# A product with w_out in seven half-size products, the activation as one ScalarE function, and a new order of the start

## The chip, the cores and the metric

One core of one Trainium2 chip runs the kernel. The metric is the device time of the whole kernel in microseconds (us), the median of several runs. All runs told here were in the fast state (executions can fall into a second, slower one, and then aren't compared). Engines are named as the profile names them: PE is TensorE, PEld its weight loads, DVE VectorE, ACT ScalarE, POOL GpSimd, SP the engine that issues most transfers.

## The reference, cut to what matters

```python
# x: (8, 3008, 256); w_in: (256, 2048); w_out: (2048, 256)
X = np.fft.fft(np.fft.fft(x, axis=1), axis=2).real        # mixing over rows, then over columns
h = X.reshape(24064, 256) @ w_in
g = h * (1.0 / (1.0 + np.exp(-1.702 * h)))                 # the quick GELU
out = g @ w_out
```

## The kernel before

The transform over the rows is done as a first stage (94 x 32 points: VectorE or GpSimd fold rows onto each other, TensorE multiplies, ScalarE copies the result out), a shuffle through DRAM, and a second stage. The transform over the columns is folded into w_in. Then 384 steps follow (8 batches, 48 each): a step makes 128 hidden units for 512 rows and their mirrored rows, and adds their product with w_out to eight accumulators. The product runs two steps behind (LAG). The first stage of the next batch is spread over the steps in 8 chunks. Below, the code is cut; `...` marks what is left out.

```python
def hidden(t):                                   # one step
    nc.tensor.matmul(pa, wcs[0][:, fs], pq[:, 0, :]); nc.tensor.matmul(pb, wcs[1][:, fs], pq[:, 1, :])
    nc.scalar.copy(v[:], pa[:])
    nc.vector.tensor_tensor(h[:, 0, :], v[:], pb[:], op=ALU.add)              # the rows
    nc.vector.scalar_tensor_tensor(dif[:], nb[:], af2[:, f:f+1], pb[:], ...)
    nc.vector.tensor_tensor(<h[:, 1, :] backwards>, v, dif, op=ALU.add)       # the mirrored rows
    nc.scalar.activation(sg[:], h[:], ACTF.Sigmoid, scale=1.702)
    nc.vector.tensor_tensor(h[:], h[:], sg[:], op=ALU.mult)

def product(t):                                  # 8 matmuls of 256 columns into 4 banks
    for sg in range(2):
        for g in range(4):
            nc.tensor.matmul(pot[2*sg + g//2][:, g % 2, :], lhsT=h[:, sg, g*128:(g+1)*128], rhs=wo[:, f, :], ...)
    # ... after 16 steps: 4 copies out of the banks, 8 stores

for t in range(n + LAG):
    if t < n: hidden(t)
    if t >= LAG: product(t - LAG)
    for fn, args in extra.get(t, ()): fn(*args)  # first stage of the next batch (a chunk every 2 steps), second stage, ...
```

In every stretch of trace shown below, an engine works through its own instructions in program order: one that could start stands behind one that can't.

## Time and profile before

| | before |
|---|---|
| time | 2282.53 us (2282.07 to 2284.93, 4 runs) |
| first step of the main loop | 122.8 us |
| a step without extras | 5.17 us |
| a batch (from one psr matmul, a small one that comes once a batch, to that of the next) | 265.5 us |

The prediction shows the lines for these. Two groups of the page of the kernel before show what the change wants to take off VectorE; columns are line, engine, operation, tiles, shapes, count, then busy us, mean ns, and the idle time before them:

```profile
L294 DVE TENSOR_TENSOR h<-h,sg 128x1024 f32<-128x1024 f32 x384 | 483.6, 1259 | 455.6 <-ACT sg L293 455.6
L293 ACT ACTIVATE sg<-h 128x1024 f32<-128x1024 f32 x384 | 405.7, 1057 | 970.2 <-DVE h L290 970.1
```

The multiply is VectorE's costliest group. Yet VectorE is busy for 60% of the span and ScalarE for 33%, and both wait for each other (455.6 and 970.1 us).

### The profile page before, as it was taken

The numbers are of one execution on the slowest core, as the hardware profiler recorded it, in microseconds if no ns is written. First come the engines' busy times: TensorE is split into PE (matmuls) and PEld (weight loads), VectorE is DVE, ScalarE is ACT, GpSimd is POOL, SyncE is SP. The second block draws the span as 40 slices with busy tenths as digits, with TensorE's granted clock in tenths as the row PEclk, the third lists the DMA queues.
The fourth block names the chain that finished last, engine by engine and source line by source line (L and its number), as shares of the span: only waits on it lengthen the run. The fifth ranks groups of instructions, "written<-read, shape, count | busy, mean of one in ns | idle before, by whom it ended". The sixth has DMA issues, their size and how long they took to land.

```text
span 2280.3 us, 21583 instructions
## 1 busy us (share of the span) xinstructions
PE 2167.9 (95%) x8496; PEld 1574.4 (69%) x8496; DVE 1358.0 (60%) x1657; ACT 748.8 (33%) x970; POOL 254.5 (11%) x277
## 2 busy tenths in 40 slices
PE   3358999999999999999999999999999999999999
PEld 2136777777777777777777777777777777777776
DVE  4255666656666556656566566565666566665665
ACT  1122333333333333333333333333333333333332
POOL 3124000310005000040003100050000400000000
PEclk9669999999999999999999999999999999999999
DMA  9700400004000130004000040001300020000000
GB/s 306 209 19 0 111 17 19 19 1 128 19 1 19 36 92 19 19 1 117 11 19 19 1 128 19 1 19 46 82 19 19 1 74 0 19 19 0 18 19 18
DMA packets 40721, 96.92 MB, mean 43 GB/s; under 512 B 4402, under 2 KB 28722, under 8 KB 38254
## 3 DMA queue, kind: packets, MB, share of 16 engines
q1 hardware_dynamic: 39536, 91.26, 14.6%
q10 hardware_dynamic: 1084, 4.29, 0.5%
q8 instruction: 66, 1.08, 0.2%
q14 instruction: 35, 0.29, 0.0%
HBM read 58.31 MB, written 48.78 MB: 47 GB/s over the span
## 4 chain that ended last, share of the span: by engine, by line
PE 89%; DVE 4%; DMA 3%; issue 2%; ACT 1%; POOL 1%; SPq 0%; DVEq 0%; ACTq 0%; POOLq 0%
PE po L305 55%; PE pa L280 14%; PE pb L281 14%; PE ps L171 2%; PE ps L197 2%; PE psn L205 1%; DMA raw<-in_moe_w_in_dram 1%; ACT sg L293 1%; DMA Xr<-in_x_dram 1%; DMA Td<-t 1%; DVE h L290 1%; DVE h L287 1%; DVE dif L289 1%; DVE os L316 0%; DVE m L240 0%
## 5 line engine op out<-in xcount | busy, mean ns | idle before, releaser
L305 PEld LDWEIGHTS po<-wo,h 128*128 128x128 f32 x6144 | 1168.0, 190 | 335.6 <-issue 134.0
L305 PE MATMUL po<-wo,h 128*128 128x256 f32 x6144 | 1393.0, 380 | 6.2 <-DVE h L294 5.1
L294 DVE TENSOR_TENSOR h<-h,sg 128x1024 f32<-128x1024 f32 x384 | 483.6, 1259 | 455.6 <-ACT sg L293 455.6
L293 ACT ACTIVATE sg<-h 128x1024 f32<-128x1024 f32 x384 | 405.7, 1057 | 970.2 <-DVE h L290 970.1
L287 DVE TENSOR_TENSOR h<-v,pb 128x512 f32<-128x512 f32 x384 | 263.8, 687 | 372.3 <-PE pb L281 369.6
L280 PE MATMUL pa<-pq,wcs 128*128 128x512 f32 x768 | 398.6, 601 | 0.0
L281 PE MATMUL pb<-pq,wcs 128*128 128x512 f32 x768 | 394.0, 595 | 1.6 <-DVE dif L289 1.6
L286 ACT COPY v<-pa 128x512 f32<-128x512 f32 x384 | 224.6, 585 | 296.6 <-PE pa L280 290.6
L289 DVE SCALAR_TENSOR_TENSOR dif<-nb,af,pb 128x512 f32<-128x512 f32 x384 | 284.6, 741 | 0.0
L290 DVE TENSOR_TENSOR h<-v,dif 128x512 f32<-128x512 f32 x384 | 268.9, 700 | 13.1
L281 PEld LDWEIGHTS pb<-pq,wcs 128*128 128x128 f32 x768 | 146.5, 191 | 187.6 <-issue 181.7
L280 PEld LDWEIGHTS pa<-pq,wcs 128*128 128x128 f32 x768 | 141.0, 192 | 38.1 <-issue 20.5
L151 POOL TENSOR_TENSOR e<-xt 94x254 f32<-94x254 f32 x7 | 5.0, 719 | 1387.2 <-DVE h L290 920.6
L171 PE MATMUL ps<-xt,w 94*96 94x256 f32 x240 | 70.2, 419 | 12.6 <-POOL xt L163 8.3
L160 POOL TENSOR_TENSOR xt<-xt 94x510 f32<-94x510 f32 (+1 forms) x59 | 73.4, 1244 | 4.6
L162 POOL TENSOR_TENSOR xt<-xt 94x254 f32<-94x254 f32 (+1 forms) x59 | 68.7, 1165 | 4.6
L176 ACT COPY t<-ps 96x512 f32<-96x512 f32 x64 | 37.2, 581 | 94.0 <-PE ps L171 93.5
L171 PEld LDWEIGHTS ps<-xt,w 94*96 94x96 f32 x240 | 42.0, 180 | 28.4 <-POOL xt L163 9.9
L261 PE MATMUL psw<-wst,small 128*128 128x512 f32 x32 | 18.7, 739 | 43.1 <-POOL wst L246 43.1
L197 PEld LDWEIGHTS ps<-small,t 128*128 128x128 f32 x384 | 51.1, 194 | 6.6 <-DVE t L189 4.2
L197 PE MATMUL ps<-small,t 128*128 128x128 f32 x384 | 51.7, 278 | 4.0 <-DVE t L189 4.0
L199 ACT COPY pq<-ps 128x512 f32<-128x512 f32 x48 | 28.1, 585 | 58.2 <-PE ps L197 58.2
(44 smaller groups left out, 344.2 us busy)
## 6 DMA issues: line engine op xcount, KB each, us to landing
out_dram<-os SPq DMA_DIRECT2D x176, 128.0 KB, 2.1
Td<-t SPq DMA_DIRECT2D x8, 1536.0 KB
t<-Td SPq DMA_DIRECT2D x8, 1536.0 KB, 7.8
Xr<-in_x_dram SPq DMA_DIRECT2D x8, 1410.0 KB, 14.4
xt<-in_x_dram SPq DMA_DIRECT2D x7, 1280.0 KB
xt<-Xr SPq DMA_DIRECT2D x7, 1200.0 KB
raw<-in_moe_w_out_dram SPq DMA_DIRECT2D x4, 1024.0 KB, 21.1
raw<-in_moe_w_in_dram ACTq DMA_DIRECT2D x3, 1024.0 KB
```

Of the source, the lines that this page charges most:

```text
L160: eng.tensor_tensor(low, low, free(t[:], up + D - 1, [-D, n], [-1, D - 1]), op=ALU.add)
L171: nc.tensor.matmul(ps[0:96, o:o + D], lhsT=w1[:, jj, :], rhs=t[:, NB - jj, :], start=True, stop=True)
L197: nc.tensor.matmul(ps[:, g * 128:(g + 1) * 128], lhsT=t4[:, 4 * blk + g, cs * H:(cs + 1) * H], rhs=m2[:, cs, :], start=True, stop=True)
L280: nc.tensor.matmul(pa[:], lhsT=wcs[0][:, fs], rhs=pq[:, 0, :], start=True, stop=True)
L281: nc.tensor.matmul(pb[:], lhsT=wcs[1][:, fs], rhs=pq[:, 1, :], start=True, stop=True)
L286: nc.scalar.copy(v[:], pa[:])
L287: nc.vector.tensor_tensor(h[:, 0, :], v[:], pb[:], op=ALU.add)
L289: nc.vector.scalar_tensor_tensor(dif[:], nb[:], af2[:, f:f + 1], pb[:], op0=ALU.mult, op1=ALU.subtract)
L290: nc.vector.tensor_tensor(free(h[:], 512 + NB - 1, [NB, 16], [-1, NB]), v[:].rearrange("p (a k) -> p a k", k=NB), dif[:].rearrange("p (a k ...
L293: nc.scalar.activation(sg[:], h[:], ACTF.Sigmoid, scale=1.702)
L294: nc.vector.tensor_tensor(h[:], h[:], sg[:], op=ALU.mult)
L305: nc.tensor.matmul(pot[2 * sg + g // 2][:, g % 2, :], lhsT=h[:, sg, g * 128:(g + 1) * 128], rhs=wo[:, f, :], start=(f == 0 and g % 2 == 0) ...
```

## The change

The intent: Strassen's scheme in Winograd's form takes seven half-size products for eight, so TensorE streams an eighth less for the product with w_out. A step now takes two blocks of 128 hidden units for half of the rows. Four sums of the activations are needed per step (s1, s3 on GpSimd, s2, s4 on VectorE), four of w_out once (wt), and seven additions when a sum ends, now every 8 steps. To make room in VectorE's time, one Gelu with the sigmoid form replaces Sigmoid and multiply. To make room in memory, the first stage writes over x. The start is put in another order: rows are turned in DRAM during the loop, a batch at a time, and not all at once, the last piece of w_in is loaded early, the first is converted before the first stage. The core of the diff:

```diff
-        nc.scalar.activation(sg[:], h[:], ACTF.Sigmoid, scale=1.702)
-        nc.vector.tensor_tensor(h[:], h[:], sg[:], op=ALU.mult)
+        nc.scalar.activation(h[:], h[:], ACTF.Gelu_apprx_sigmoid)
+
+    def sums(t):                                  # called for t - 1 in hidden(t), after the first half of h
+        a11, a12, a21, a22 = h[:, 0, 0, :], h[:, 0, 1, :], h[:, 1, 0, :], h[:, 1, 1, :]
+        nc.gpsimd.tensor_tensor(s1, a21, a22, op=ALU.add)
+        nc.gpsimd.tensor_tensor(s3, a11, a21, op=ALU.subtract)
+        nc.vector.tensor_tensor(s2, s1, a11, op=ALU.subtract)
+        nc.vector.tensor_tensor(s4, a12, s2, op=ALU.subtract)
 
     def product(t):
-            ... 8 matmuls of 256 columns
+        plan = ((0, 0, h[:, 0, 0, :], wo[:, p, 0, :]), (0, 1, s[:, 1, :], wt[:, p, 1, :]),
+                ... )                             # seven, each as two matmuls of 128 columns
+        ...                                       # when a sum ends:
+        nc.scalar.copy(c1[:], m1)
+        for out, i0, i1, o in ((u2[:], c1[:], m6, ALU.add), ... ):      # seven
+            nc.vector.tensor_tensor(out, i0, i1, op=o)
...
-    for b in range(1, B):
-        turn(b, 17, 32)                           # at the start
+        if b + 2 < B:
+            at(t0 + 10, turn, b + 2, 17, 32)      # in the loop
...
-                at(t0 + 3 + 2 * c, stage1, b + 1, c, nc.gpsimd)
+                at(t0 + 7 + 2 * c, stage1, b + 1, c, nc.gpsimd)
```

(Left out: the early load and conversion of w_in, the in-place copy of the first stage, the split of the shuffle, buffer counts.)

More of the change, by code (lines that the diff above doesn't have):

```diff
@@ L93 @@
     xp = ctx.enter_context(tc.tile_pool(name="xp", bufs=1, space=SB))
-    tp = ctx.enter_context(tc.tile_pool(name="tp", bufs=2, space=SB))
+    tp = ctx.enter_context(tc.tile_pool(name="tp", bufs=1, space=SB))
     pqp = ctx.enter_context(tc.tile_pool(name="pqp", bufs=2, space=SB))
@@ L112 @@
     wcs = [const.tile([128, DF], F32, tag=f"wcs{i}", name=f"wcs{i}") for i in range(2)]
-    wo = const.tile([128, NF, D], F32, tag="wo", name="wo")
+    wo = const.tile([128, NF // 2, 4, H], F32, tag="wo", name="wo")
+    wt = const.tile([128, NF // 2, 4, H], F32, tag="wt", name="wt")
     af2 = const.tile([128, NF], F32, tag="af2", name="af2")
@@ L118, in bank @@
         return psm.tile([128, 512], F32, tag="mm", name=name)
-    xt, t1t, t4t, pqt, nbt = {}, {}, {}, {}, {}
+    xt, t4t, pqt, nbt = {}, {}, {}, {}
     def turn(b, m0, m1):
@@ L129, in load_x @@
     def load_x(b, pieces=((0, 16),)):
-        t = xt[b] = xp.tile([NA, NB, D], F32, tag="x", name="xt")
+        t = xt[b] = xp.tile([96, NB, D], F32, tag="x", name="xt")
         src = x[b].rearrange("(p j) d -> p j d", j=NB)
@@ L144, in stage1 @@
     def stage1(b, c, eng):
-        t = xt[b]
+        full = xt[b]
+        t = full[0:NA]
         if c == 0:
             e = sp.tile([NA, 2, D], F32, tag="v", name="e")
-            fwd, rev = free(t[:], 1, [16 * D, 2], [1, H - 1]), free(t[:], D - 1, [16 * D, 2], [-1, H - 1])
+            fwd, rev = free(t, 1, [16 * D, 2], [1, H - 1]), free(t, D - 1, [16 * D, 2], [-1, H - 1])
             eng.tensor_tensor(e[:, :, 1:H], fwd, rev, op=ALU.add)
-            eng.tensor_copy(free(e[:], 0, [D, 2], [H, 2]), free(t[:], 0, [16 * D, 2], [H, 2]))
+            eng.tensor_copy(free(e[:], 0, [D, 2], [H, 2]), free(t, 0, [16 * D, 2], [H, 2]))
             eng.tensor_tensor(e[:, :, H + 1:D], fwd, rev, op=ALU.subtract)
@@ L156, in stage1 @@
         at, up = lo * D, (NB - lo) * D
-        ends = free(t[:], up, [-D, n], [H, 2])
-        eng.tensor_tensor(ends, ends, free(t[:], at, [D, n], [H, 2]), op=ALU.add)
-        low = free(t[:], at + 1, [D, n], [1, D - 1])
-        eng.tensor_tensor(low, low, free(t[:], up + D - 1, [-D, n], [-1, D - 1]), op=ALU.add)
-        fwd, rev = free(t[:], at + 1, [D, n], [1, H - 1]), free(t[:], at + D - 1, [D, n], [-1, H - 1])
-        eng.tensor_tensor(free(t[:], up + 1, [-D, n], [1, H - 1]), fwd, rev, op=ALU.add)
-        eng.tensor_tensor(free(t[:], up + H + 1, [-D, n], [1, H - 1]), fwd, rev, op=ALU.subtract)
-        if c == 0:
-            t1t[b] = tp.tile([96, 16, D], F32, tag="t1", bufs=1, name="t1")
+        ends = free(t, up, [-D, n], [H, 2])
+        eng.tensor_tensor(ends, ends, free(t, at, [D, n], [H, 2]), op=ALU.add)
+        low = free(t, at + 1, [D, n], [1, D - 1])
+        eng.tensor_tensor(low, low, free(t, up + D - 1, [-D, n], [-1, D - 1]), op=ALU.add)
+        fwd, rev = free(t, at + 1, [D, n], [1, H - 1]), free(t, at + D - 1, [D, n], [-1, H - 1])
+        eng.tensor_tensor(free(t, up + 1, [-D, n], [1, H - 1]), fwd, rev, op=ALU.add)
+        eng.tensor_tensor(free(t, up + H + 1, [-D, n], [1, H - 1]), fwd, rev, op=ALU.subtract)
         ps = bank("ps1")
@@ L175, in stage1, with spill, fill @@
                 nc.tensor.matmul(ps[0:96, c0:c1], lhsT=w1[:, l1, :], rhs=e[:, 1, c0:c1], start=False, stop=True)
-        nc.scalar.copy(t1t[b][:, 2 * c:2 * c + 2, :].rearrange("p j d -> p (j d)"), ps[0:96, :])
-    def shuffle(b):
+        nc.scalar.copy(full[:, 2 * c:2 * c + 2, :].rearrange("p j d -> p (j d)"), ps[0:96, :])
+    def spill(b):
+        nc.sync.dma_start(out=Td[b].rearrange("(p j) d -> p j d", j=16), in_=xt[b][:, 0:16, :])
+    def fill(b):
         t4 = t4t[b] = tp.tile([128, NG, D], F32, tag="t4", name="t4")
-        nc.sync.dma_start(out=Td[b].rearrange("(p j) d -> p j d", j=16), in_=t1t[b][:])
         nc.sync.dma_start(out=t4[:], in_=Td[b].rearrange("(a p) d -> p a d", p=128))
@@ L226, in bounds @@
         hi = raw[key][:, :, 1].bitcast(F32)
-        g = sp.tile([128, 1024], F32, tag="sg", name="g")
+        g = sp.tile([128, 1024], F32, tag="s", bufs=3, name="g")
         m = cv.tile([128, 1024], F32, tag="m", bufs=2, name="m")
@@ L254, in round_out @@
     def round_out(n):
-        rounded(wo[:, 4 * n:4 * n + 4, :].rearrange("p f n -> p (f n)"), ("out", n))
+        ps = slice(2 * n, 2 * n + 2)
+        rounded(wo[:, ps].rearrange("p f q n -> p (f q n)"), ("out", n))
+        b11, b12, b21, b22 = (wo[:, ps, q, :] for q in range(4))
+        t1, t2, t3, t4 = (wt[:, ps, q, :] for q in range(4))
+        for out, i0, i1 in ((t1, b12, b11), (t2, b22, t1), (t3, b22, b12), (t4, t2, b21)):
+            nc.gpsimd.tensor_tensor(out, i0, i1, op=ALU.subtract)
     def fold_w(n):
@@ L269, in nyquist_weights @@
         nc.vector.tensor_scalar(af2[:], ps[:, 0:NF], scalar1=2.0, scalar2=None, op0=ALU.mult)
-    steps = [(b, blk, f) for b in range(B) for blk in range(NBLK) for f in range(NF)]
-    ht, pot = {}, {}
+    NP = NF // 2
+    steps = [(b, blk, hh, p) for b in range(B) for blk in range(NBLK) for hh in range(2) for p in range(NP)]
+    ht, st, pot, ot = {}, {}, {}, {}
     def hidden(t):
-        b, blk, f = steps[t]
-        pq, nb, fs = pqt[b, blk], nbt[b, blk], slice(f * 128, (f + 1) * 128)
+        b, blk, hh, p = steps[t]
+        pq, nb, ks = pqt[b, blk], nbt[b, blk], slice(hh * 256, hh * 256 + 256)
         pa, pb = bank("pa"), bank("pb")
-        nc.tensor.matmul(pa[:], lhsT=wcs[0][:, fs], rhs=pq[:, 0, :], start=True, stop=True)
-        nc.tensor.matmul(pb[:], lhsT=wcs[1][:, fs], rhs=pq[:, 1, :], start=True, stop=True)
-        h = ht[t] = hp.tile([128, 2, 512], F32, tag="h", name="h")
+        for ps, cs in ((pa, 0), (pb, 1)):
+            for i in range(2):
+                f = 2 * p + i
+                nc.tensor.matmul(ps[:, i * 256:(i + 1) * 256], lhsT=wcs[cs][:, f * 128:(f + 1) * 128],
+                                 rhs=pq[:, cs, ks], start=True, stop=True)
+        h = ht[t] = hp.tile([128, 2, 2, 256], F32, tag="h", name="h")
         v = sp.tile([128, 512], F32, tag="v", name="v")
-        sg = sp.tile([128, 2, 512], F32, tag="sg", name="sg")
+        dif = sp.tile([128, 512], F32, tag="dif", name="dif")
         nc.scalar.copy(v[:], pa[:])
-        nc.vector.tensor_tensor(h[:, 0, :], v[:], pb[:], op=ALU.add)
-        dif = sp.tile([128, 512], F32, tag="dif", name="dif")
-        nc.vector.scalar_tensor_tensor(dif[:], nb[:], af2[:, f:f + 1], pb[:], op0=ALU.mult, op1=ALU.subtract)
+        nc.vector.tensor_tensor(h[:, 0].rearrange("p f k -> p (f k)"), v[:], pb[:], op=ALU.add)
+        sums(t - 1)
+        for i in range(2):
+            c = slice(i * 256, i * 256 + 256)
+            f = 2 * p + i
+            nc.vector.scalar_tensor_tensor(dif[:, c], nb[:, ks], af2[:, f:f + 1], pb[:, c],
+                                           op0=ALU.mult, op1=ALU.subtract)
         nc.vector.tensor_tensor(free(h[:], 512 + NB - 1, [NB, 16], [-1, NB]),
@@ L292, in hidden @@
                                 dif[:].rearrange("p (a k) -> p a k", k=NB), op=ALU.add)
-        nc.scalar.activation(sg[:], h[:], ACTF.Sigmoid, scale=1.702)
-        nc.vector.tensor_tensor(h[:], h[:], sg[:], op=ALU.mult)
+        nc.scalar.activation(h[:], h[:], ACTF.Gelu_apprx_sigmoid)
+    def sums(t):
+        if not 0 <= t < len(steps):
+            return
+        h = ht[t]
+        s = st[t] = sp.tile([128, 4, 256], F32, tag="s", bufs=3, name="s")
+        a11, a12, a21, a22 = h[:, 0, 0, :], h[:, 0, 1, :], h[:, 1, 0, :], h[:, 1, 1, :]
+        s1, s2, s3, s4 = (s[:, q, :] for q in range(4))
+        nc.gpsimd.tensor_tensor(s1, a21, a22, op=ALU.add)
+        nc.gpsimd.tensor_tensor(s3, a11, a21, op=ALU.subtract)
+        nc.vector.tensor_tensor(s2, s1, a11, op=ALU.subtract)
+        nc.vector.tensor_tensor(s4, a12, s2, op=ALU.subtract)
@@ L296, in product @@
     def product(t):
-        b, blk, f = steps[t]
-        if f == 0:
+        b, blk, hh, p = steps[t]
+        if p == 0:
             for n in range(4):
-                pot[n] = pso.tile([128, 2, D], F32, tag=f"o{n}", name=f"po{n}")
-        h = ht.pop(t)
-        for sg in range(2):
-            for g in range(4):
-                nc.tensor.matmul(pot[2 * sg + g // 2][:, g % 2, :], lhsT=h[:, sg, g * 128:(g + 1) * 128],
-                                 rhs=wo[:, f, :], start=(f == 0 and g % 2 == 0), stop=(f == NF - 1),
-                                 skip_group_check=True)
@@ L308, in product @@
-        if f < NF - 1:
-            return
-        for sg in range(2):
-            o = op.tile([128, 4, D], F32, tag="os", name="os")
-            for i in range(2):
-                dst = free(o[:], 3 * D - 2 * i * D, [-D, 2], [1, D]) if sg else o[:, 2 * i:2 * i + 2, :]
-                eng = nc.scalar.copy if i else nc.vector.tensor_copy
-                eng(dst, pot[2 * sg + i][:])
-            store(b, blk, sg, o)
+                pot[n] = pso.tile([128, 2, 2, H], F32, tag=f"o{n}", name=f"po{n}")
@@ new lines, in product @@
+        h, s = ht.pop(t), st.pop(t)
+        plan = ((0, 0, h[:, 0, 0, :], wo[:, p, 0, :]), (0, 1, s[:, 1, :], wt[:, p, 1, :]),
+                (1, 0, h[:, 0, 1, :], wo[:, p, 2, :]), (1, 1, s[:, 2, :], wt[:, p, 2, :]),
+                (2, 0, s[:, 0, :], wt[:, p, 0, :]), (2, 1, s[:, 3, :], wo[:, p, 3, :]),
+                (3, 0, h[:, 1, 1, :], wt[:, p, 3, :]))
+        for n, i, lhs, rhs in plan:
+            for q in range(2):
+                nc.tensor.matmul(pot[n][:, i, q, :], lhsT=lhs[:, q * 128:(q + 1) * 128], rhs=rhs,
+                                 start=(p == 0 and i == 0 and q == 0), stop=(p == NP - 1), skip_group_check=True)
@@ new lines, in product @@
+        if p < NP - 1:
+            return
+        (m1, m6), (m2, m7), (m5, m3), (m4, _) = ((pot[n][:, 0], pot[n][:, 1]) for n in range(4))
+        if hh == 0:
+            for sg in range(2):
+                ot[sg] = op.tile([128, 4, D], F32, tag="os", name="os")
+        c1, u2, u3, u4 = (op.tile([128, 2, H], F32, tag=f"u{n}", bufs=1, name=f"u{n}") for n in range(4))
+        dst = [ot[0][:, 2 * hh:2 * hh + 2, :], free(ot[1][:], (3 - 2 * hh) * D, [-D, 2], [1, D])]
+        nc.scalar.copy(c1[:], m1)
@@ new lines, in product @@
+        for out, i0, i1, o in ((u2[:], c1[:], m6, ALU.add), (dst[0][:, :, 0:H], c1[:], m2, ALU.add),
+                               (u3[:], u2[:], m7, ALU.add), (u4[:], u2[:], m5, ALU.add),
+                               (dst[0][:, :, H:], u4[:], m3, ALU.add), (dst[1][:, :, H:], u3[:], m5, ALU.add),
+                               (dst[1][:, :, 0:H], u3[:], m4, ALU.subtract)):
+            nc.vector.tensor_tensor(out, i0, i1, op=o)
+        if hh:
+            for sg in range(2):
+                store(b, blk, sg, ot[sg])
@@ L333 @@
     nc.scalar.dma_start(out=small[:], in_=tab2)
+    load_in(0, nc.scalar)
     for p0, p1 in PIECES:
@@ L336 @@
     nc.vector.memset(ones[:], 1.0)
-    for n in range(3):
+    for n in range(1, 3):
         load_in(n, nc.scalar)
-    for b in range(1, B):
-        turn(b, 17, 32)
     bounds(("in", 0))
     bounds(("in", 1))
+    round_in(0)
     for c in range(NCH):
         stage1(0, c, nc.gpsimd if c in (1, 4, 6) else nc.vector)
-    shuffle(0)
-    if B > 1:
-        load_x(1)
-    for n in range(NCK):
+    load_in(3, nc.sync)
+    spill(0)
+    fill(0)
+    fold_w(0)
+    bounds(("in", 2))
+    for n in range(1, NCK):
         round_in(n)
-        if n == 0:
-            load_in(3, nc.sync)
-        else:
-            load_out(n - 1, nc.sync)
+        load_out(n - 1, nc.sync)
         bounds(("in", n + 2) if n + 2 < NCK else ("out", n + 2 - NCK))
@@ L358 @@
     load_out(3, nc.sync)
+    if B > 1:
+        turn(1, 17, 32)
+        load_x(1)
     rotate(0)
@@ L370 @@
     for i in range(1, NCK):
-        at(3 * i - 3, round_out, i)
+        at(2 * i - 2, round_out, i)
         if i + 1 < NCK:
-            at(3 * i - 3, bounds, ("out", i + 1))
+            at(2 * i - 2, bounds, ("out", i + 1))
     for b in range(B):
         t0 = b * NBLK * NF
+        if b + 2 < B:
+            at(t0 + 10, turn, b + 2, 17, 32)
         if b + 1 < B:
             for c in range(NCH):
-                at(t0 + 3 + 2 * c, stage1, b + 1, c, nc.gpsimd)
-            at(t0 + 20, shuffle, b + 1)
+                at(t0 + 7 + 2 * c, stage1, b + 1, c, nc.gpsimd)
+            at(t0 + 24, spill, b + 1)
+            at(t0 + 29, fill, b + 1)
             if b + 2 < B:
-                at(t0 + 20, load_x, b + 2)
+                at(t0 + 33, load_x, b + 2)
             at(t0 + 38, rotate, b + 1)
@@ L392 @@
             hidden(t)
+        if t == n:
+            sums(n - 1)
         if t >= LAG:
```

## The prediction

> **What bounds the kernel now.** I read the page's busy times and groups first, then the timeline of single steps in the middle, then the timeline of the start. A step is one pass of the main loop (384 of them: 8 batches, 48 each).
>
> ```profile
> span 2280.3 us, 21583 instructions
> PE 2167.9 (95%) x8496; PEld 1574.4 (69%) x8496; DVE 1358.0 (60%) x1657; ACT 748.8 (33%) x970; POOL 254.5 (11%) x277
> PE 89%; DVE 4%; DMA 3%; issue 2%; ACT 1%; POOL 1%; SPq 0%; DVEq 0%; ACTq 0%; POOLq 0%
> L305 PE MATMUL po<-wo,h 128*128 128x256 f32 x6144 | 1393.0, 380 | 6.2 <-DVE h L294 5.1
> ```
>
> TensorE is the bound: 89% of the chain that ended last. It waits 6 us in all for the activation (last line). The groups overlap, so I take rates from start times in the timeline:
>
> ```profile
> 380.02 1.05 PE L197 MATMUL ps<-small,t 128*128 128x128 f32 x8
> 380.91 1.02 PE L280 MATMUL pa<-pq,wcs 128*128 128x512 f32 x2
> 381.77 1.02 PE L281 MATMUL pb<-pq,wcs 128*128 128x512 f32 x2
> 382.63 3.62 PE L305 MATMUL po<-wo,h 128*128 128x256 f32 x16
> 386.08 1.02 PE L280 MATMUL pa<-pq,wcs 128*128 128x512 f32 x2
> ```
>
> A step is 386.08 - 380.91 = 5.17 us: 0.86 for pa, 0.86 for pb, 3.45 for the product with w_out (16 records, since each fp32 matmul is two: 216 ns each). The eight L197 records have 128 moving columns, each with its own weights: 0.89 / 8 = 111 ns. That is the very shape of the new product. A batch, taken from one psr matmul to the next (369.46 to 635.00), is 265.5 us.
>
> The start is a second part. The first step begins at 122.8 us, and before it TensorE stands still for a DMA:
>
> ```profile
> 93.71 1.11 POOL L230 TENSOR_SCALAR m<-raw 128x1024 f32<-128x1024 f32 x1 [34.96 <-DMA raw<-in_moe_w_in_dram]
> ...
> 97.18 5.17 PE L261 MATMUL psw<-wst,small 128*128 128x512 f32 x8 [34.67 <-POOL wst L246]
> ```
>
> The last piece of w_in is queued behind the turning of seven batches and the load of x for batch 1.
>
> **What the Trainium skill says.** "TensorE: Matmul & The Clock Gate", section "LDWEIGHTS (loading the stationary operand)": a load takes its column count over 1.2 GHz, 107 ns for 128 columns. The trace agrees: 32 matmuls of one column (L267) took 3.64 us, 114 ns a pair. So loads just fit behind 128-column matmuls, with nothing to spare. The same page, "What's actually happening", says the clock halves after an idle window of about 3.4 us. The trace agrees: after 7.74 us of idle, four L171 records took 2.02 us against 1.03, while a gap of 2.05 us left the next 16 products at 3.69. "SBUF — State Buffer", section "SBUF: two separate sides", says that a VectorE operation with two SBUF inputs and a GpSimd operation exclude each other for a whole instruction. The start shows it:
>
> ```profile
> 32.95 1.43 POOL L160 TENSOR_TENSOR xt<-xt 94x510 f32<-94x510 f32 x1
> 33.18 1.48 DVE L163 TENSOR_TENSOR xt<-xt 94x254 f32<-94x254 f32 x1
> ```
>
> L163 takes 0.41 us elsewhere on VectorE; here it ends 0.28 us after GpSimd does. "ScalarE: Activation LUTs" ("The pipeline for one element" and what follows) says that all functions cost the same per element; so I keep the Sigmoid's 1.06 us for the Gelu. Only the changed kernel can show that.
>
> **The change, part by part.**
>
> TensorE: the product becomes 14 matmuls of 128 columns, 28 records at 111 to 114 ns, say 112: 3.14 us for 3.45. The hidden product has 8 records of 256 columns at 216 ns, 1.73, as before. A step is then 4.87 us: 0.30 x 384 = 115 us saved if nothing else waits. (By columns alone it would be an eighth of 3.45, 0.43.)
>
> VectorE: the multiply by the sigmoid (1.26 us) goes. Added per step are s2 and s4, 0.42 each (the 94x254 operation on VectorE), and one more fixed part of splitting the 741 ns operation (267 ns of it is half the elements at 0.96 GHz, an estimate), 0.2. So VectorE's load stays at about 3.2 us. At each end of a sum, now 48 and not 24, come 7 operations of 0.4, 2.8 us, behind one ScalarE copy.
>
> The cycle through the engines is new. From the end of one Gelu: s1 on GpSimd 0.72 and s3 until 1.43 (94x254 on GpSimd is 719 ns); s2 is held by the lock until s3 is done, ends at 1.71; s4 to 2.17, two halves to 2.95, second half of h to 3.68, Gelu from 3.77 to 4.83. So this cycle takes 4.83 us against TensorE's 4.87: two bounds at once. The lag of two steps hides latency but no shortage of rate; the 2.8 us at each sum's end is not wholly made up for. I charge 0.9 us per end for banks that are read late (before: 16.1 us in 23 ends, 0.7 each).
>
> GpSimd and the first stage, where I expect the loss. GpSimd works in order:
>
> ```profile
> 198.80 0.21 POOL L158 TENSOR_TENSOR xt<-xt 94x4 f32<-94x4 f32 x1
> 199.08 1.26 POOL L160 TENSOR_TENSOR xt<-xt 94x510 f32<-94x510 f32 x1
> 200.42 0.72 POOL L162 TENSOR_TENSOR xt<-xt 94x254 f32<-94x254 f32 x1
> 201.11 0.72 POOL L163 TENSOR_TENSOR xt<-xt 94x254 f32<-94x254 f32 x1
> ```
>
> A chunk is 3.0 us undisturbed; the means of the four groups in the middle of the run (403, 1315, 1261, 832 ns) sum to 3.8. Before, GpSimd had only this and ran all chunks ahead of TensorE. Now chunk c stands behind s1 and s3 of the step before. With step t starting at 0, the Gelu of t-1 ends at about 1.3, s1 and s3 are done at 2.75, the chunk at 5.75 to 7.1 with the lock. TensorE comes to its matmuls at 4.87: a wait of 0.9 to 2.3, say 1.9 us, 8 times in 7 batches. It is short enough for the clock to stay up.
>
> A batch then: 48 x 4.87 = 233.8; first-stage matmuls 8 x 0.87 = 7.0; second stage 6 x 0.89 = 5.3; the broadcast row 3 x 1.05 = 3.2; sum ends 6 x 0.9 = 5.4; chunk waits 8 x 1.9 = 15.2. Together 269.9 against 265.5: no gain in the steady part. The last batch lacks first stage and waits: 247.7.
>
> The start: without the turns in the way the last piece of w_in is there by about 35 us. VectorE then strings four conversions (5.0 us each; the first is now done while x is on its way) after the first stage's end at 42: 47, 58, 63 with the waits for ScalarE, then folding and row sums (3.7 us each) to 73, conversion of w_out to 79, second stage and broadcast: step 0 at about 83, 40 us earlier. In the first steps before, 75 us (122.8 to 197.7) held 8 steps and 3 chunks, which at full rate are 44: 31 us lost, by GpSimd and VectorE strung behind the conversions of w_out. Now chunks start at step 7, but a GpSimd conversion carries four subtractions more: I say 17 lost.
>
> The sum: 83 + 17 + 7 x 269.9 + 247.7 + 9 (evacuation and stores) = 2246 for the profile's span, and 3 more for the time. I place the middle a little lower, at 2235, since the chunk wait is the term that I trust least, and the loads without collisions would make it half.
>
> **The rivals.** *The chunk waits are small.* If the wait is 0.9 us, a batch is 261.9 and the time about 2193, -4%. For it: the operations of VectorE with two SBUF inputs get fewer (s2, s4, h: 1.5 us a step against 1.9). Against: order alone gives 0.9, since no chunk can pass s1. *The cycle becomes the bound.* If each of its five hand-overs costs 0.05 us more, a step is about 5.1, which is the step of before; with the chunk waits overlapping, the time is about 2290. For it: 4.83 leaves no room for the sums' ends. Against: single operations overlap by about 0.08 in the trace. *Loads become the bound.* At 125 ns a pair the step would be 5.23 and the time above 2370; L197 and L267 speak against it. *All columns pay*: no waits at all gives 2246 - 106 = 2140, and I find nothing that takes the order of GpSimd away.
>
> **Range and chances.** The start gives about 54 us with some certainty, 2.4%. The steady part is between -8 and +5 us a batch for seven batches. That makes 2165 to 2300 the range for 8 in 10. The threshold of 2% is at 2237, almost at my middle: faster 0.50, same 0.39, slower 0.11.
>
> **What would show it.** Product records spaced 111 to 114 ns; the first step near 83 us; TensorE idle 1 to 2.3 us before each first-stage matmul, put down to GpSimd's L163 equivalent, some 110 us in all; stalls of about 0.9 us at sum starts; ScalarE at 1.06 us for the Gelu; a batch period of 262 to 272. I am wrong if the batch period is below 258 (GpSimd's order does not bind) or above 280 (the cycle, or the loads, bind).

## The result, and the profile after

The changed kernel takes 2248.62 us (2246.96 to 2249.73) against 2282.53. The ratio is 0.9849, 95% interval 0.9832 to 0.9866. Ratios here are the mean time of one kernel's fast runs over that of the other's of the same rounds, so not quite the ratio of the medians quoted.

The page of the changed kernel: span, busy time per engine, the chain that ended last, and one group of the product with its weight loads.

```profile
span 2247.0 us, 36224 instructions
...
PE 2072.1 (92%) x14640; PEld 1915.1 (85%) x14640; DVE 1375.7 (61%) x2713; ACT 694.8 (31%) x970; POOL 782.9 (35%) x1061
...
PE 35%; DVE 35%; POOL 10%; issue 10%; ACT 8%; DMA 2%; ACTq 0%; DVEq 0%; SPq 0%; POOLq 0%
...
L341 PE MATMUL po<-wo,h 128*128 128x128 f32 x3072 | 473.6, 277 | 26.6 <-DVE u L356 26.5
L341 PEld LDWEIGHTS po<-wo,h 128*128 128x128 f32 x3072 | 432.5, 192 | 60.0 <-DVE u L356 41.5
```

TensorE's busy time fell by 96 us, but the span by 33. The chain is no longer TensorE's: 89% became 35%, with VectorE and GpSimd in it. Where it went shows in the psr matmuls, which mark the batches: the first two of the main loop are at 334.19 and 600.35 in the changed kernel, at 369.46 and 635.00 before. So 35.3 us are won before the first of them, and from there to the end 1912.8 us pass against 1910.8: the steady part is 2 us slower. Over five batches, a batch is (1934.95 - 600.35) / 5 = 266.9 us.

The step itself is as short as the prediction worked out (4.87 us). In the timeline of the changed kernel in a stretch without extras (start, duration, engine, line, operation; in brackets the idle time before and what ended it):

```profile
382.88 1.03 PE L296 MATMUL pa<-pq,wcs 128*128 128x256 f32 x4
383.34 1.06 ACT L313 ACTIVATE h<-h 128x1024 f32<-128x1024 f32 x1 [3.42 <-DVE h L310]
384.53 0.73 POOL L323 TENSOR_TENSOR s<-h 128x256 f32<-128x256 f32 x1 [3.53 <-issue]
385.22 0.73 POOL L324 TENSOR_TENSOR s<-h 128x256 f32<-128x256 f32 x1
385.51 0.71 DVE L325 TENSOR_TENSOR s<-s,h 128x256 f32<-128x256 f32 x1
...
386.26 0.42 DVE L326 TENSOR_TENSOR s<-h,s 128x256 f32<-128x256 f32 x1
...
387.73 1.03 PE L296 MATMUL pa<-pq,wcs 128*128 128x256 f32 x4
388.28 1.06 ACT L313 ACTIVATE h<-h 128x1024 f32<-128x1024 f32 x1 [3.41 <-DVE h L310]
```

TensorE's step is 387.73 - 382.88 = 4.85 us. But from Gelu to Gelu it is 388.28 - 383.34 = 4.94 us: the cycle through ScalarE, GpSimd and VectorE is longer than TensorE's step, and falls behind by 0.09 a step. DVE L325 (s2) shows the lock, as I call the exclusion of VectorE and GpSimd that the prediction describes: s2 takes 0.71 us and ends 0.27 us after GpSimd's s3, while s4 (L326), an operation of the same size that runs when GpSimd is still, takes 0.42.

And the timeline of the changed kernel around one chunk of the first stage:

```profile
1005.21 0.73 POOL L324 TENSOR_TENSOR s<-h 128x256 f32<-128x256 f32 x1
1005.89 0.42 POOL L164 TENSOR_TENSOR xt<-xt 94x4 f32<-94x4 f32 x1
...
1006.39 1.44 POOL L166 TENSOR_TENSOR xt<-xt 94x510 f32<-94x510 f32 x1
...
1007.90 1.05 POOL L168 TENSOR_TENSOR xt<-xt 94x254 f32<-94x254 f32 x1
...
1008.92 0.72 POOL L169 TENSOR_TENSOR xt<-xt 94x254 f32<-94x254 f32 x1
1009.60 0.72 POOL L323 TENSOR_TENSOR s<-h 128x256 f32<-128x256 f32 x1
...
1009.69 1.10 PE L175 MATMUL ps<-xt,w 94*96 94x256 f32 x4 [1.46 <-POOL xt L169]
```

The chunk starts only after s3 of the step before, takes 3.75 us (3.0 undisturbed, 3.4 in the mean of the run), and TensorE stands still for 1.46 us until it is done. Two lines of the waits of the changed kernel (who waited for whom, us in total, times, longest) give the sum:

```profile
PE ps L175 <- POOL xt L169: 63.3, 42, 1.6
...
PE po L341 <- DVE u L356: 26.5, 33, 2.3
```

The second is the wait at the ends of sums; counted at the weight loads, which come first, it is 41.5 us. The third loss is at the start of the loop (the first of these two lines is VectorE's own wait):

```profile
105.28 0.93 DVE L325 TENSOR_TENSOR s<-s,h 128x256 f32<-128x256 f32 x1 [6.60 <-POOL s L323]
...
106.26 1.22 PE L341 MATMUL po<-wt,s 128*128 128x128 f32 x4 [11.25 <-DVE s L325]
```

The first step begins at 87.24 us, and three waits of TensorE of 11.25, 7.75 and 6.41 us for s2 follow in the first six steps. In each, VectorE has ended its part of a conversion of w_out and is idle itself, for 6.60, 6.61 and 5.54 us, until GpSimd has made s1: that stands behind GpSimd's part of the conversion, an integer addition of 2.38 us and four subtractions of 0.72 (in two of the three also a clamp of 1.09).

### The profile page after: what moved, and what is told of

Same layout as the page of the kernel before. It is cut to its first block, busy times and chain, and to the rows that moved or that the text cites. A ratio compares the mean times of both kernels' runs of the same rounds, so it can differ in the third digit from the quotient of the medians.

```text
span 2247.0 us, 36224 instructions
## 1 busy us (share of the span) xinstructions
PE 2072.1 (92%) x14640; PEld 1915.1 (85%) x14640; DVE 1375.7 (61%) x2713; ACT 694.8 (31%) x970; POOL 782.9 (35%) x1061
## 4 chain that ended last, share of the span: by engine, by line
PE 35%; DVE 35%; POOL 10%; issue 10%; ACT 8%; DMA 2%; ACTq 0%; DVEq 0%; SPq 0%; POOLq 0%
PE po L341 17%; DVE dif L308 8%; DVE h L303 7%; PE pa L296 6%; DVE h L310 6%; PE pb L296 6%; DVE s L325 5%; DVE s L326 4%; ACT v L302 4%; ACT h L313 3%; POOL xt L166 3%; PE ps L175 2%; POOL xt L168 2%; DVE u L356 1%; POOL s L324 1%
## 5 line engine op out<-in xcount | busy, mean ns | idle before, releaser
L313 ACT ACTIVATE h<-h 128x1024 f32<-128x1024 f32 x384 | 405.8, 1057 | 1403.0 <-DVE h L310 1379.1
L323 POOL TENSOR_TENSOR s<-h 128x256 f32<-128x256 f32 x384 | 279.3, 727 | 1363.9 <-issue 988.7
L341 PE MATMUL po<-wt,s 128*128 128x128 f32 x4608 | 647.2, 277 | 26.5 <-DVE s L325 26.5
L341 PEld LDWEIGHTS po<-wt,s 128*128 128x128 f32 x4608 | 582.6, 193 | 27.6 <-DVE s L325 27.3
L341 PE MATMUL po<-wo,h 128*128 128x128 f32 x3072 | 473.6, 277 | 26.6 <-DVE u L356 26.5
L341 PEld LDWEIGHTS po<-wo,h 128*128 128x128 f32 x3072 | 432.5, 192 | 60.0 <-DVE u L356 41.5
L296 PE MATMUL pa<-pq,wcs 128*128 128x256 f32 x1536 | 401.0, 384 | 0.0
L296 PE MATMUL pb<-pq,wcs 128*128 128x256 f32 x1536 | 396.6, 381 | 0.0
L308 DVE SCALAR_TENSOR_TENSOR dif<-nb,af,pb 128x256 f32<-128x256 f32 x768 | 332.1, 473 | 0.0
L324 POOL TENSOR_TENSOR s<-h 128x256 f32<-128x256 f32 x384 | 279.8, 729 | 0.0
L341 PE MATMUL po<-wo,s 128*128 128x128 f32 x1536 | 235.1, 276 | 0.0
L325 DVE TENSOR_TENSOR s<-s,h 128x256 f32<-128x256 f32 x384 | 217.8, 567 | 20.8 <-POOL s L323 20.8
L326 DVE TENSOR_TENSOR s<-h,s 128x256 f32<-128x256 f32 x384 | 178.2, 464 | 13.1
L175 PE MATMUL ps<-xt,w 94*96 94x256 f32 x240 | 73.5, 433 | 68.4 <-POOL xt L169 63.3
```

The costliest lines, as they stand in the source:

```text
L175: nc.tensor.matmul(ps[0:96, o:o + D], lhsT=w1[:, jj, :], rhs=t[:, NB - jj, :], start=True, stop=True)
L296: nc.tensor.matmul(ps[:, i * 256:(i + 1) * 256], lhsT=wcs[cs][:, f * 128:(f + 1) * 128], rhs=pq[:, cs, ks], start=True, stop=True)
L308: nc.vector.scalar_tensor_tensor(dif[:, c], nb[:, ks], af2[:, f:f + 1], pb[:, c], op0=ALU.mult, op1=ALU.subtract)
L313: nc.scalar.activation(h[:], h[:], ACTF.Gelu_apprx_sigmoid)
L323: nc.gpsimd.tensor_tensor(s1, a21, a22, op=ALU.add)
L324: nc.gpsimd.tensor_tensor(s3, a11, a21, op=ALU.subtract)
```

## The experiments

My theory: the gain of 34 us is the start's alone; the seven products save what was expected on TensorE (0.32 us a step), and lose it in waits that come from the order of GpSimd and ScalarE. The rivals: the cycle of 4.94 us takes the gain whatever the order; the lock does; or the seven products do contribute and something else costs.

| run | base and edit | median us | ratio to before |
|---|---|---|---|
| e5_start | before, only the order of the start | 2235.76 | 0.9792 |
| e4_gelu | before, only the Gelu | 2268.19 | 0.9932 |
| e11_no_seven | before, both of these | 2216.99 | 0.9713 |
| (the change) | all | 2248.62 | 0.9849 |
| e1_split | change, first-stage matmuls one step later | 2212.98 | 0.9692 |
| e2_early | change, product before Gelu | 2198.70 | 0.9629 |
| e3_both | change, both | 2138.59 | 0.9372 |
| e8_start | e3_both, conversions on GpSimd later | 2132.32 | 0.9345 |
| e10_half | change, Gelu in two calls | 2171.90 | 0.9518 |
| e9_half | e8_start, Gelu in two calls | 2109.71 | 0.9240 |
| e6_dve | change, s1 and s3 on VectorE | 2346.26 | 1.0283 |
| e7_sigmoid | change, Sigmoid and multiply back | 2695.78 | 1.1816 |

All gave correct results. Each was timed in three rounds against the kernel before on the same chip.

**The start alone (e5_start).** The kernel before with the new order of the start:

```diff
-    for b in range(1, B):
-        turn(b, 17, 32)
+    (first piece of w_in loaded before w1 and converted before the first stage; last piece loaded after it; shuffle and load of x moved as well)
+            at(t0 + 10, turn, b + 2, 17, 32)
-                at(t0 + 3 + 2 * c, stage1, b + 1, c, nc.gpsimd)
+                at(t0 + 7 + 2 * c, stage1, b + 1, c, nc.gpsimd)
```

> The kernel before with only the order of the start: turns one batch ahead, first piece of w_in converted before the first stage, last piece loaded right after it, first stage of the next batch from step 7. Theory (the whole gain of the change lies before the first steady batch, 35 us by the traces, and the steady part is even): 2235 to 2250, so as fast as the full change or faster, since no subtractions for the seven products stand in its way. Rival (the seven products give a part of the gain): 2260 or more.

Measured: 2235.76 us. This part alone is 13 us faster than the whole change. Its first step begins at 87.17 us, as in the changed kernel, and its batch stays at 265.5 us. Its first psr matmul of the loop is at 323.09 us, against 369.46 before: of these 46.4 us, 35.6 are won before the first step and 10.8 after it, in the first steps. The latter are missing in the changed kernel (334.19).

**The Gelu alone (e4_gelu).**

```diff
-        nc.scalar.activation(sg[:], h[:], ACTF.Sigmoid, scale=1.702)
-        nc.vector.tensor_tensor(h[:], h[:], sg[:], op=ALU.mult)
+        nc.scalar.activation(h[:], h[:], ACTF.Gelu_apprx_sigmoid)
```

> The kernel before with one Gelu in place of Sigmoid and multiply, nothing else. Theory (TensorE is the bound at 5.17 us a step, VectorE's 1.26 us a step lie beside it): the same within 5 us, 2278 to 2283. Rival (VectorE's release of h was a hidden cost): 2240 or less.

Measured: 2268.19 us, 15 us faster, outside what either side expected. Of that, 9 us lie before the first psr matmul of the loop (360.60 against 369.46), where VectorE has conversions to do as well, and most of the rest in a batch of 264.9 us for 265.5. In the steady step VectorE's multiply did lie beside TensorE, as the theory had it; the start I had left out. The traces of the first steps show it: waits of TensorE of 2.05 and 3.03 us for the multiply, the second followed by 16 product records in 6.23 us for 3.62, became one of 1.71 us, and a wait for GpSimd of 7.74 us became 4.47.

**Start and Gelu, no seven products (e11_no_seven).** The edits of the last two together.

> The kernel before with the order of the start and the Gelu together: the change without its seven products. Theory (the seven products, as they stand in the changed kernel, give back in waits more than they save): the two gains add up, 47 + 15 us, but part of the 15 lies in the first steps, which the start shortens as well: 2215 to 2235 us, 13 to 33 us faster than the full change. Rival (the seven products pay for themselves): 2248 or more.

Measured: 2216.99 us. So the seven products, as they stand in the change, cost 2248.62 - 2216.99 = 32 us, together with what they bring along (the in-place copy and the split shuffle, fewer buffers, conversions of w_out every two steps and not three). The rival that they pay for themselves is out. Where they cost it, the traces tell: the first psr matmul of the loop is at 309.22 us here and at 334.19 in the changed kernel, so 25 us are lost before it, 24 of them by the start of the ninth step (135.66 against 159.66), and only 7 in the rest (1905.8 us against 1912.8). In the steady part the seven products are about even.

**The first stage's matmuls one step later (e1_split).** The sums on GpSimd are issued where they were; only TensorE's part moves:

```diff
-                at(t0 + 7 + 2 * c, stage1, b + 1, c, nc.gpsimd)
+                at(t0 + 7 + 2 * c, stage1_sums, b + 1, c, nc.gpsimd)
+                at(t0 + 8 + 2 * c, stage1_mm, b + 1, c)
```

> The changed kernel with the first stage's matmuls issued one step after its sums on GpSimd, nothing else. Theory (the matmuls stand behind sums that GpSimd's order holds back: 1.46 us at each of 56 chunks in the trace of the changed kernel): the waits go, the batch period falls from 266.5 to about 254 us and the time to about 2165 us. Rival 1 (the cycle Gelu - s1 - s2 - dif - h - Gelu, 4.94 us in the trace, takes over as soon as the waits no longer give it time): a part of the gain comes back as waits for the seven sums at each end; 2190 to 2215. Rival 2 (the lock between the two engines, not the order): no change, 2245.

Measured: 2212.98 us, a batch of 262.0 us. The waits for GpSimd are gone from the main loop, so rival 2 as stated, no change, is out: a later place for the matmuls is enough. What made the sums late is not parted by this run, since a step of slack hides both the order and the 0.75 us by which the chunk shown above is longer than undisturbed; an estimate from that chunk is half each (with 3.0 us it would have left 0.7 of the 1.46). For the order speaks e6_dve below. But rival 1 came true: from the waits of this run,

```profile
PE po L350 <- DVE u L365: 62.7, 47, 2.7
```

The 26.5 us at the ends of sums became 62.7. My reading is that the chunk waits had given the cycle time to catch up; without them it is behind at 47 of the 48 ends of a sum, and TensorE waits there.

**The product before the Gelu (e2_early).** In the same step, so that ScalarE's copy of m1 stands before the Gelu and not behind it:

```diff
+        if t >= LAG:
+            product(t - LAG)
         nc.scalar.activation(h[:], h[:], ACTF.Gelu_apprx_sigmoid)
```

> The changed kernel with the product issued before the Gelu of the same step, so that the one ScalarE copy at the end of a sum stands ahead of the Gelu in ScalarE's order. Theory (TensorE waits at 33 to 39 of the 48 sum ends for additions that stand behind that copy, 26 to 40 us in all): 2248 falls by 20 to 35 us, to about 2220, and the waits for the additions are gone from the trace. Rival (the additions themselves, 2.8 us on VectorE, set the wait): under 8 us.

Measured: 2198.70 us, 50 us less, a batch of 260.7 us. The wait for the additions no longer appears among TensorE's longest, and VectorE's own wait for the copy of m1 fell from 67.7 to 0.7 us. The gain is that of the theory and larger: it corresponds to the 41.5 us counted at the weight loads, and the chunk waits fell with it, from 63.3 to 54.7 us in the main group. The additions' own 2.8 us were not what TensorE waited for; it was where they started.

**Both (e3_both).**

> Both edits in the changed kernel: first-stage matmuls one step after their sums, and the product issued before the Gelu. Theory (two separate waits, so that what the first edit lost to sum ends comes back): the matmul waits (54.7 us where only the product was moved) and the waits for the additions (62.7 us where only the first stage was split) are both gone; batch period 252 to 255 us, time 2140 to 2165 us. Rival (the cycle of 4.94 us a step takes all of it): not under 2190.

Measured: 2138.59 us, a batch of 252.2 us. The two edits alone give 36 and 50 us, together 110: what the first lost at the ends of sums comes back. TensorE's waits for the additions are down to 12.0 us. The rival is out: the cycle is as long as before, but 48 times 4.94 us are 237, under the 252 us of a batch, so it has time to catch up between the ends of sums. And the seven products now pay: e11_no_seven, with the same start and Gelu, takes 78 us more. From the first psr matmul of the loop (322.53) to the end, 1814.7 us pass against 1905.8, 91 less, of which the first steps still take 13 back. The shorter step alone would give 0.32 x 346 = 111 us there.

**Conversions later (e8_start).** On e3_both; GpSimd's integer addition of each conversion of w_out one step later, the four subtractions two steps later:

```diff
-        at(2 * i - 2, round_out, i)
+        at(2 * i - 2, round_out, i, True)          # VectorE's part only
+        at(2 * i - 1, rounded_add, ("out", i))
+        at(2 * i, round_sums, i)
```

> Both edits, and in the first steps GpSimd's part of each conversion of w_out issued one step later (the subtractions two steps later), so that it does not stand in front of s1 while it waits for VectorE. Theory (the three waits of 11.3, 7.8 and 6.4 us for s2 in the first six steps come from GpSimd's order, too): 12 to 22 us less than with both edits alone. Rival (VectorE's own conversions, 5 us each, set these waits): within 5 us of both edits alone.

Measured: 2132.32 us, 6 us less, nearer to the rival. The waits for s2 fell from 26.0 to 18.0 us, so part of them was GpSimd's order. In the three waits that remain, 5.85, 5.37 and 5.67 us, VectorE no longer waits for s1. Its own conversion fills about half of each; most of the rest is s2 itself, held by the lock, which neither side had named:

```profile
99.55 2.36 POOL L270 TENSOR_TENSOR wo<-a,g 128x1024 uint32<-128x1024 uint32 x1 [2.42 <-DVE a L261]
...
99.99 2.21 DVE L349 TENSOR_TENSOR s<-s,h 128x256 f32<-128x256 f32 x1
```

Beside GpSimd's integer addition, s2 takes 2.21 us for 0.42.

**s1 and s3 on VectorE (e6_dve).**

```diff
-        nc.gpsimd.tensor_tensor(s1, a21, a22, op=ALU.add)
-        nc.gpsimd.tensor_tensor(s3, a11, a21, op=ALU.subtract)
+        nc.vector.tensor_tensor(s1, a21, a22, op=ALU.add)
+        nc.vector.tensor_tensor(s3, a11, a21, op=ALU.subtract)
```

> The changed kernel with s1 and s3 on VectorE instead of GpSimd: no order on GpSimd and no lock is left to hold anything up, but the cycle from one Gelu to the next gets longer by two operations. Theory of the cycle: from the trace of the changed kernel 4.94 - 0.29 (lock) + two more starts of about 0.35 = 5.3 to 5.4 us a step; that is above TensorE's 4.85 and its slack of two steps can't make up a rate, so the time rises to 2280 to 2340. Rival (only the load of each engine counts: VectorE then has 4.1 us a step, under 4.85): the first-stage waits go and the time falls to about 2170.

Measured: 2346.26 us, 98 us slower than the change, a little beyond the theory's range. In its timeline, in a quiet stretch:

```profile
700.69 1.06 ACT L313 ACTIVATE h<-h 128x1024 f32<-128x1024 f32 x1 [3.73 <-DVE h L310]
...
705.95 1.06 ACT L313 ACTIVATE h<-h 128x1024 f32<-128x1024 f32 x1 [3.73 <-DVE h L310]
```

The cycle is 5.26 us, and VectorE's share of the span is only 68%. That is the cycle at work, not a load: the first-stage waits are down to 5.4 us in all, and the kernel is slower all the same, with 144.3 us of waits at the ends of sums. The 5.4 us also bear on e1_split: GpSimd has no s1 and s3 before a chunk any more, while the lock is still there. What it is over the range lies in the steps with a chunk, where some of VectorE's sums run beside GpSimd's and take up to 0.95 us for 0.42.

**Sigmoid and multiply put back (e7_sigmoid).**

```diff
-        nc.scalar.activation(h[:], h[:], ACTF.Gelu_apprx_sigmoid)
+        nc.scalar.activation(sg[:], h[:], ACTF.Sigmoid, scale=1.702)
+        nc.vector.tensor_tensor(h[:], h[:], sg[:], op=ALU.mult)
```

> The changed kernel with Sigmoid and multiply put back for the Gelu. Theory of the cycle: 1.2 us more in it, 6.1 us a step and some 300 us a batch: 2500 to 2620 us, though the same swap in the kernel before was worth 15 us. Rival (VectorE's load of 4.5 us a step still lies beside TensorE's 4.85): under 2290.

Measured: 2695.78 us. The quiet step, again from its timeline, is 810.64 - 804.40 = 6.24 us, against 6.1 expected:

```profile
804.40 1.06 ACT L314 ACTIVATE sg<-h 128x1024 f32<-128x1024 f32 x1 [4.71 <-DVE h L310]
...
810.64 1.06 ACT L314 ACTIVATE sg<-h 128x1024 f32<-128x1024 f32 x1 [4.70 <-DVE h L310]
```

The rest over the range is waits that grew with it (TensorE for the additions 192.6 us, for the chunks 126.6). The swap is worth 15 us without the seven products and 447 with them: VectorE's busy time mattered little in the kernel before; its place in the cycle does now.

**The Gelu in two calls (e10_half).** On the changed kernel:

```diff
         nc.vector.tensor_tensor(<h[:, 0]>, v[:], pb[:], op=ALU.add)
+        nc.scalar.activation(h[:, 0], h[:, 0], ACTF.Gelu_apprx_sigmoid)
...
-        nc.scalar.activation(h[:], h[:], ACTF.Gelu_apprx_sigmoid)
+        nc.scalar.activation(h[:, 1], h[:, 1], ACTF.Gelu_apprx_sigmoid)
```

> The changed kernel with the Gelu in two calls: the first half of h right after it is made, the second half where the whole was. Theory (order: s1 and the copy at a sum's end both start when the last Gelu call ends, and that is now about 0.45 us earlier, half of the elements): each first-stage wait and most sum ends get up to 0.45 us shorter, 8 x 0.45 + 6 x 0.45 = 6 us a batch, 45 us in all, about 2200 us. Rival (one more ScalarE operation a step costs as much as it brings): within 8 us of the changed kernel.

Measured: 2171.90 us, 77 us less, well over the 45. In its timeline, where it catches up after the end of a sum:

```profile
392.08 0.63 ACT L314 ACTIVATE h<-h 128x512 f32<-128x512 f32 x1 [1.91 <-DVE h L311]
...
396.54 0.63 ACT L314 ACTIVATE h<-h 128x512 f32<-128x512 f32 x1 [1.91 <-DVE h L311]
```

The cycle is now 4.46 us, under TensorE's 4.85, though ScalarE does more work (797.5 us busy for 694.8). So it can catch up after each disturbance, which the estimate of 0.45 us a wait had left out: TensorE's waits for the additions are gone, and the main group of those for the chunks fell from 63.3 to 39.8 us. ScalarE's half call takes 0.63 us and leaves only that half in the cycle.

**The same on e8_start (e9_half).**

> The kernel with both edits and the later conversions, and the Gelu in two calls. The waits that the earlier end could shorten are mostly gone there (13 us for the additions, 18 us at the start), and TensorE's own work is 252 us a batch. So a small gain, 0 to 15 us: 2117 to 2132 us.

Measured: 2109.71 us, 0.9240 of before (0.9224 to 0.9255). It beats both kernels and every other run. From the first psr matmul of the loop (309.84) to the end, 1797.2 us pass, 109 less than in e11_no_seven and nearly all of the 111 that the shorter step can give. Its chain is TensorE's again:

```profile
PE 93%; DVE 3%; DMA 2%; POOL 1%; issue 1%; ACT 0%; SPq 0%; DVEq 0%; ACTq 0%; POOLq 0%
```

## Why the prediction was right or wrong

The time was within the range, 14 us over the stated middle of 2235 and equal to the sum that the prediction worked out (2246 for the span, measured 2247.0). By 2% it is "same", to which it had given 0.39, less than to "faster". And the sum is not as good as it looks: two of its terms are off by some 20 us each, in opposite directions. That they cancel is luck.

- **Product at 111 to 114 ns a record: right.** The step is 4.85 us, taken as 4.87. The loads did not bind. The Gelu takes the Sigmoid's 1.06 us (1057 ns in the mean), as said.
- **No gain in the steady part: right. From GpSimd's order: right in kind.** e1_split takes the chunk waits away by issuing the matmuls later. Mis-sized: 1.9 us a chunk was said; 63.3 and 7.0 us (the chunk of each batch with the e tile) over 56 chunks are 1.26. The part of the order alone was said to be 0.9; the chunk shown gives about 0.7, an estimate.
- **Sum ends at 0.9 us: right in size.** 41.5 us at the weight loads over 48 ends are 0.86. The mechanism is right in half: the prediction put the seven additions behind one ScalarE copy, but charged the wait to their 2.8 us. e2_early shows that the place of the copy, behind the Gelu, makes it.
- **The cycle beside TensorE's step: right, 0.11 us too short.** 4.83 was said, 4.94 measured. The missing 0.11 is the hand-over from ScalarE to GpSimd: the Gelu ends at 384.40 and s1 starts at 384.53, where the working had nothing between. So it was not "two bounds at once": the cycle was the longer one, and e1_split paid for that.
- **A batch of 269.9 us: measured 266.9**, inside 262 to 272. Seven batches make this 21 us too much.
- **The start: half right.** The first step was said to be near 83 us and was at 87.24. The failed term is "I say 17 lost" in the first steps. From 87.24 to the ninth step's start at 159.66, 72.4 us pass for eight steps and one chunk, which at 4.85 and 0.87 us are 39.7: 33 lost. The prediction counted the four subtractions more on GpSimd, and they do stand in front of s1; but it does not say that s2, and TensorE with it, now waits until a conversion is through on VectorE and then on GpSimd. In e5_start, which has no s1, TensorE's waits for the activation are 7.4 us in all; here three waits for s2 make up 25.4 us, VectorE is idle for s1 for 18.8 us of that time, and after each TensorE's records take twice as long at first (1.22 us for 0.61). So the start's gain was 35 us, not 54; without the seven products it was 46 (e5_start).
- **Chance.** Moving the middle from the worked 2246 down to 2235, because the chunk wait might be half, was a guess. The wait was smaller, as guessed, but the loss at the start took it back.
- **"I find nothing that takes the order of GpSimd away": wrong.** The matmuls could be issued a step later with the sums where they were.
- **The clock after a gap: true of the two gaps shown, not as a threshold.** The same trace has a gap of 3.03 us, under 3.4, after which the granted clock is 0.58 (16 product records in 6.23 us); in e5_start it is 0.67 after 2.58 us, in e1_split 1.00 after 2.68. The chunk waits were shorter (1.6 us at most), so nothing in the sum rests on it.

What stays open: why e4_gelu gains 9 us at the start was read from the traces and not tested by itself; what the in-place first stage and the fewer buffers cost was not tested apart from the seven products (e9_half leaves them little); and how the remaining 18 us of waits for s2 in the first steps divide between VectorE's conversions and the lock.

## What to carry to other kernels

Before splitting work over more engines to shorten the bound engine's instructions, add up the cycle from one step's activation to the next through all engines: over a batch it must leave time to catch up. At 5.26 and 6.24 us a step (e6_dve, e7_sigmoid) it set the time in spite of the lag of two steps; at 4.94 it was bearable only once the orders were mended (e3_both); at 4.46 TensorE's waits for the additions went down to 0.2 us (e9_half). When an engine gets a second job with waits in it, look at what else stands in its order, and issue the consumers of that work a step later. Test the parts of a compound change alone, and look where in the run each gains: here one part won 47 us and another gave 32 back, 25 of them in the first steps.

## What the Trainium skill lacked or had wrong

- "Perfetto Trace Analysis", section "Identifying the Most-Contended Engine", says to optimize the engine with the highest occupancy first. In e7_sigmoid that is still TensorE (82% busy, its weight loads 75%, VectorE 71%), yet a step takes 6.24 us where TensorE needs 4.85. A cycle through several engines, added up as a bound, is on no page that I read.
- "TensorE: Matmul & The Clock Gate", section "LDWEIGHTS (loading the stationary operand)", has a formula that makes 107 ns for 128 columns (an estimate); the trace has 114 a pair. The page lacks a measured duration of fp32 records with a new weight load for each: here each matmul is two records, of 111 ns at 128 columns and 216 ns at 256, sustained over whole steps.
- The same page, section "What's actually happening", has the clock halve after an idle window of about 3.4 us. The runs show a lower clock after gaps of 3.03 us (0.58, kernel before) and 2.58 us (0.67, e5_start), and the full clock after one of 2.68 us (e1_split).
- "SBUF — State Buffer", section "SBUF: two separate sides", has the lock, but not how it looks in a profile: not as idle time, but as a longer operation (0.71 us for 0.42, ending 0.27 us after the other engine).
- No page that I read has the hand-over from ScalarE to GpSimd: 0.13 us from the Gelu's end to the start of s1.
